# Expert rows loaded from GpSimd's queue, scatters without waits on each other, and the last block's low parts on VectorE

## The chip, the cores and the metric

The kernel runs on one core of a Trainium2 chip. The metric is the device time of one execution in microseconds (us). Engine names follow the profile: PE is TensorE's matmul stream (PEld its weight loads), DVE is VectorE, ACT is ScalarE, POOL is GpSimd, SP is SyncE, which does no arithmetic here and only issues transfers (SPq is its queue of instructions).

## The reference

Three layers follow each other on 3072 tokens of width 512:

```python
x  = attention(q, k, v)            # 4 batches, 8 heads, 768 tokens, head width 64, local window and global keys
h  = x @ w_in                      # 512 -> 2048
x  = (h - tanh(h)) @ w_out         # 2048 -> 512
e  = argmax(x @ w_gate, axis=1)    # each token goes to one of 8 experts
out[e == i] = gate_w * eom * (relu(x[e == i] @ w1[i]) @ w2[i])    # 512 -> 1024 -> 512
```

## The kernel before, in words

Every fp32 factor of a large matmul is held as a high and a low part, and each product is three matmuls (high by high, high by low, low by high), so most values that PE needs are written twice: the high part by ACT, the low part by a subtraction.

**First half.** The tokens go in 12 blocks of 256 (`blk` 0 to 11). For each block and each of 16 slices `u` of the hidden width, `moe_h` makes `ph` on PE, `gate` and `gate2` make `gg` on DVE and ACT, `parts` makes `gh` (ACT) and `gl` (line 645: DVE in block 0, POOL in all later blocks), and `moe_y` adds the slice into `y`. Attention of later blocks is woven in between. After a block its two halves of 128 rows are copied to `yrow` (buffers of the pool tag `row`, of which there are three), routed (`rt_logits`: `step1` to `step5`, with the rank matmuls `rk`, and the row numbers `su`), and written by `scatter` (line 793, an indirect DMA issued by POOL) to `srt`, a table in device memory that is sorted by expert. Each scatter of blocks 0 to 10 waits until the scatter before it has landed; the two of block 11 don't wait for each other.

**Second half.** `order_experts` ranks the experts by load, and nine jobs follow: job 0 is the first 256 rows of the fullest expert, which block 10 has already completed, job 1 its other 256 rows, and jobs 2 to 8 are the other experts, with 480 to 384 rows each. `ex_load` brings a piece of an expert's weights (`ex`, 512 KB, SP's queue, into the same `row` buffers), `ex_split` makes its high part `eh` on ACT (line 899) and its low part `el` on DVE (line 900). `ex_rows` (line 923) brings a job's sorted rows, `xr`, 128 at a time, on SP's queue too. `ex_T` turns them on PE (`xTp`, line 941) and splits them (`xTh` on ACT, `xTl` on DVE); `ex_s1` makes `h2p` and its parts `h2h` and `h2l`; `ex_s2` adds into `ob` (line 1000); `ex_out` scales `ob` to `orow` and POOL writes it to its places in `out` (line 1018, an indirect DMA).

**Order.** Each engine runs its instructions strictly in the order that the compiler of the kernel fixed beforehand, from the order of the code, ranks in an agenda and estimated times. An instruction that must wait therefore holds up all that stand behind it on its engine. This holds for SP's and POOL's transfers as well: a transfer that waits for a buffer or for another transfer keeps the next one from being issued.

Of the kernel before, what the change touches and what calls it, by code (L numbers as in the profile page):

```python
# [32 lines left out]
def kernel(  # L33
# [15 lines left out]
    nc = tc.nc  # L49
    P = 128  # L50
# [3 lines left out]
    E, _, F = w1.shape  # L54
    TB = 256
    NBLK = NT // TB
# [8 lines left out]
    RS = NT + CAP  # L65
# [14 lines left out]
    srt = dram.tile([E * RS, W], F32, name="srt")  # L80
# [11 lines left out]
    def bank(tag, bufs, name):  # L92
        t = psum.tile([P, 512], F32, tag=tag, bufs=bufs, name=name)
        return t
# [17 lines left out]
    order_i = persist.tile([P, E], I32, name="order_i")  # L112
# [19 lines left out]
    def at(gt, rank, fn):  # L132
        agenda.setdefault((gt, rank), []).append(fn)
# [465 lines left out]
    def moe_h(blk, u, gt):  # L599
        fg, fo = divmod(u, 4)  # L600
        ph = bank("h", 2, f"ph{blk}_{u}")
        n = 0
        for kc in range(KC):
            o = kc * 512 + fo * P
            whi, wlo = wih[fg][:, o : o + P], wil[fg][:, o : o + P]
            for lw, xx in ((whi, xhi), (whi, xlo), (wlo, xhi)):
                nc.tensor.matmul(ph[:, 0:TB], lw, xx[blk][:, kc, :], start=(n == 0), stop=(n == 3 * KC - 1))  # L607
                n += 1

        def tmp(tag, bufs, dt=F32):  # L610
            t = p1.tile([P, TB], dt, tag=tag, bufs=bufs, name=f"{tag}{blk}_{u}")
            return t

        L = {}

        def gate():
            hps = ph[:, 0:TB]
            uu = L["uu"] = tmp("uu", 2)
            ss = L["ss"] = tmp("ss", 2)
            tt = L["tt"] = tmp("tt", 2)  # L620
            vv = L["vv"] = tmp("vt", 2)
            nc.scalar.activation(uu, hps, AF.Square)  # L622
            nc.scalar.activation(tt, hps, AF.Tanh)  # L623
            nc.scalar.activation(ss, uu, AF.Square, scale=G_S, bias=ga[:, 0:1])  # L624
            nc.vector.scalar_tensor_tensor(out=vv, in0=uu, scalar=G_C, in1=hps, op0=ALU.add, op1=ALU.mult)  # L625
            nc.vector.tensor_tensor(out=tt, in0=tt, in1=hps, op=ALU.subtract)  # L626
            nc.vector.scalar_tensor_tensor(out=vv, in0=ss, scalar=G_S2B, in1=vv, op0=ALU.add, op1=ALU.mult)

        def gate2():
            uu, ss, tt, vv = L["uu"], L["ss"], L["tt"], L["vv"]  # L630
            gg = L["gg"] = tmp("gg", 2)
            if blk < 1:
                nc.scalar.activation(ss, uu, AF.Relu, bias=nt2[:, 0:1])
            else:
                nc.vector.tensor_scalar(out=ss, in0=uu, scalar1=G_T2, scalar2=None, op0=ALU.is_gt)
            nc.vector.tensor_tensor(out=gg, in0=vv, in1=uu, op=ALU.mult)
            nc.vector.copy_predicated(gg, ss.bitcast(I32), tt)  # L637

        def parts():
            gg = L["gg"]  # L640
            gh = tmp("gh", 3, F32R)
            gl = tmp("gl", 3, F32R)
            nc.scalar.copy(gh, gg)  # L643
            by = nc.vector if blk < 1 else nc.gpsimd
            by.tensor_tensor(out=gl, in0=gg, in1=gh.bitcast(F32), op=ALU.subtract)  # L645
            g_t[blk, u] = (gh, gl)

        at(gt + 1, 0, gate)
        at(gt + 2, 0, gate2)
        at(gt + 3, 0, parts)  # L650

    def moe_y(blk, u):
# [14 lines left out]


    rts = {}
    last_rows = []  # L670

    def rt_evac(blk):
        for j in range(2):
# [24 lines left out]
    def rt_logits(blk, gt):  # L698
# [92 lines left out]
        def scatter(j):  # L791
            r = rts.pop((blk, "row", j))
            store = nc.gpsimd.indirect_dma_start(
                out=srt[:, :], out_offset=IndirectOffsetOnAxis(ap=L["su"][:, j : j + 1], axis=0),
                in_=r[:, 0:W], in_offset=None, bounds_check=E * RS - 1, oob_is_err=False,
            )
            if blk == NBLK - 1:
                last_rows.append(store.ins)
                if j == 1:
                    tc.declare_no_dep(last_rows[1], last_rows[0], reason="each token has one row")  # L800

        last = blk == NBLK - 1
        rk = -2 if last else 0
# [4 lines left out]
        at(gt + 3, rk, step4)  # L808
        at(gt + 3, rk, step5)
        at(gt + 4, rk, lambda: scatter(0))  # L810
        at(gt + (4 if last else 6), rk, lambda: scatter(1))

    def plan_route(blk, gt):
# [21 lines left out]
    ordering = {}  # L835
# [25 lines left out]
        nc.vector.tensor_scalar(out=kk, in0=kk, scalar1=-1.0, scalar2=float(E), op0=ALU.mult, op1=ALU.add)  # L861
        nc.vector.tensor_copy(order_i, kk)

    def expert(r):

        if r not in ordering:
            ordering[r] = nc.values_load(
                order_i[0:1, r : r + 1], engines=[mybir.EngineType.SP], min_val=0, max_val=E - 1
            )
        return ordering[r]  # L870


    w1h, w1l, w2h, w2l = {}, {}, {}, {}
# [3 lines left out]
    def ex_load(e, i):  # L877
        st = rowt(f"ex{e}_{i}")
        rv = expert(e)
        if i < 4:  # L880
            nc.sync.dma_start(st, w1[ds(rv, 1), i * P : (i + 1) * P, :].rearrange("o p f -> p (o f)"))
        else:
            r = (i - 4) * 2 * P
            nc.sync.dma_start(
                st.rearrange("p (c d) -> p c d", c=2),
                w2[ds(rv, 1), r : r + 2 * P, :].rearrange("o (c p) d -> p (o c) d", p=P),
            )
        staged["e", e, i] = st
# [24 lines left out]
    def job_tile(n, tag, shape, dt, name):  # L913
        pool, tag, bufs = pools[tag, 0 if n == 0 else 2 - n % 2]
        t = pool.tile(shape, dt, tag=tag, bufs=bufs, name=name)
        return t

    def ex_rows(n):
        r, j0, _ = jobs[n]
        rv = expert(r)  # L920
        for j, m in tiles(n):
            t = job_tile(n, "xr", [P, W], F32, f"xr{n}_{j}")
            nc.sync.dma_start(t[0:m, :], srt[ds(rv * RS + (j0 + j) * P, m), :])
            xrows[n, j] = t

    def tiles(n):

        return [(j, min(P, jobs[n][2] - j * P)) for j in range((jobs[n][2] + P - 1) // P)]
# [259 lines left out]
    for i in range(NP):  # L1188
# [5 lines left out]
        ("orow", 0): (persist, "row", 3),  # L1194
    })
    at(G + 26, 0, lambda: ex_rows(0))
    for g in range(n_groups(0)):
        at(G + 28 + g, 4, lambda g=g: ex_T(0, g))
# [48 lines left out]
    for k in range(1, 3):  # L1247
        pools["hh", k] = p2, "h2h", 3
        pools["hl", k] = p2, "h2l", 3
        pools["orow", k] = p2, "orow", 4  # L1250

    ex_rows(1)
    for g in range(n_groups(1)):
        ex_T(1, g)
    for n in range(1, len(jobs)):
        e = jobs[n][0]
        for f in range(NF2):
            ex_s1(n, f)
            if n == 1:
                for i in range(NP):  # L1260
                    if steps[i] - NF2 == f:
                        ex_load(1, i)
                    if steps[i] + 2 - NF2 == f and i >= 4:
                        ex_split(1, i)
            elif e + 1 < E:
                ex_load(e + 1, f)
                if f >= 1:
                    ex_split(e + 1, f - 1)
            if f >= 1:
                if n < len(jobs) - 1 or f - 1 < NF2 - LATE:  # L1270
                    ex_s2(n, f - 1)
            elif n > 1:
                ex_s2(n - 1, NF2 - 1)
                ex_out(n - 1)
            if n + 1 < len(jobs):
                if f == 2:
                    ex_rows(n + 1)
                if 4 <= f < 4 + n_groups(n + 1):
                    ex_T(n + 1, f - 4)
                if f == NF2 - 1 and n > 1:  # L1280
                    ex_split(e + 1, NP - 1)
# [95 lines left out]
def build(shapes):  # L1377
    import numpy as _np
    import concourse.bacc as _bacc
    import concourse.tile as _tile  # L1380
    from concourse import mybir as _mybir

    nc = _bacc.Bacc("TRN2", target_bir_lowering=False, num_devices=1)
    args = []
    for name in _INS:
        shape, dtype = shapes[name]
        args.append(
            nc.dram_tensor(f"in_{name}_dram", shape, _mybir.dt.from_np(_np.dtype(dtype)), kind="ExternalInput").ap()
        )
    for i, (shape, dtype) in enumerate(_OUTS):  # L1390
        dt = _mybir.dt.from_np(_np.dtype(dtype))
        args.append(nc.dram_tensor(f"out_{i}_dram", shape, dt, kind="ExternalOutput").ap())
    with _tile.TileContext(nc, schedule_with_timeline_sim=True) as tc:
        kernel(tc, *args)
    return nc
# [23 lines left out]
```

## Time and profile before

| | |
|---|---|
| three runs | 1169.68, 1170.34, 1171.40 us (median 1170.34) |
| profiled execution, its own time | 1168.82 us |
| its span, first to last instruction | 1167.1 us |
| busy in the span | PE 1106.7, DVE 856.2, ACT 671.6, POOL 214.2 us |
| mean granted TensorE clock | 0.988 of 2.4 GHz |

The profile is of one execution, and its times count from the start of the span. The first half ends at about 815 us and the second follows up to 1155 us. A row of the timeline gives start, duration, engine, source line, operation, output <- inputs, and in square brackets how long the engine had been idle before it and what ended that. A granted clock of 1.00 is 2.4 GHz and 0.50 is 1.2 GHz.

### The profile page before, as it was taken

How to read it: one execution, taken by the hardware profiler on the slowest of the kernel's cores; microseconds unless marked ns; L12 is line 12 of the kernel's file. 1: busy time of each engine (PE TensorE's matmuls, PEld its weight loads, DVE VectorE, ACT ScalarE, POOL GpSimd, SP SyncE). 2: the span in 40 equal slices, each digit the busy share in tenths (PEclk: the TensorE clock that was granted, in tenths of full speed). 3: DMA queues.
4: the chain of work that ended last, by engine and by line, in shares of the span. 5: the costliest groups of instructions: out<-in, count | busy, mean ns of one | idle time of the engine just before them, and what ended most of it. 6: DMA issues, size and time to landing. Idle time of an engine off the chain costs nothing. (4 is left out here: it accounts for less than half of the span.)

```text
span 1167.1 us, 22211 instructions
## 1 busy us (share of the span) xinstructions
PE 1106.7 (95%) x7374; PEld 943.5 (81%) x7374; DVE 856.2 (73%) x2704; ACT 671.6 (58%) x1794; POOL 214.2 (18%) x281
## 2 busy tenths in 40 slices
PE   2888999999999999999999999998999999999995
PEld 1457888888888888888888888886888787888894
DVE  6899778899989889989889898998554434424411
ACT  4999876666666656666666666565352423423411
POOL 1000013222222222222222232324100100101100
PEclk9889999999999999999999999999999999999998
DMA  6954921111211112121112120113372614526200
GB/s 170 291 165 142 254 58 42 30 51 30 55 38 40 37 39 52 31 55 27 51 24 56 37 53 22 33 67 127 113 246 103 206 53 153 181 61 222 79 23 25
DMA packets 128850, 103.25 MB, mean 88 GB/s; under 512 B 101679, under 2 KB 101679, under 8 KB 128720
## 3 DMA queue, kind: packets, MB, share of 16 engines
q1 hardware_dynamic: 124592, 89.06, 26.7%
q0 software_dynamic: 4128, 12.61, 2.8%
q8 instruction: 62, 1.02, 0.4%
q14 instruction: 68, 0.56, 0.2%
HBM read 90.04 MB, written 21.88 MB: 96 GB/s over the span
## 5 line engine op out<-in xcount | busy, mean ns | idle before, releaser
L645 POOL TENSOR_TENSOR gl<-gg,gh 128x256 fp32r<-128x256 f32 x176 | 149.1, 847 | 485.7 <-ACT gh L643 368.1
L607 PE MATMUL ph<-xhi,wh 128*128 128x256 f32 x768 | 219.9, 289 | 3.5 <-DVE tt L626 3.5
L607 PE MATMUL ph<-xhi,wl 128*128 128x256 f32 x768 | 218.2, 285 | 0.0
L607 PE MATMUL ph<-xlo,wh 128*128 128x256 f32 x768 | 216.2, 282 | 0.0
L662 PE MATMUL y<-wh,gh 128*128 128x512 f32 x384 | 158.2, 412 | 1.0 <-ACT gh L643 0.9
L607 PEld LDWEIGHTS ph<-xhi,wh 128*128 128x128 f32 x768 | 144.8, 189 | 15.9 <-DVE tt L626 5.9
L662 PE MATMUL y<-wl,gh 128*128 128x512 f32 x384 | 154.1, 401 | 0.0
L607 PEld LDWEIGHTS ph<-xlo,wh 128*128 128x128 f32 x768 | 145.0, 189 | 6.7
L607 PEld LDWEIGHTS ph<-xhi,wl 128*128 128x128 f32 x768 | 144.8, 189 | 4.3 <-issue 2.6
L662 PE MATMUL y<-wh,gl 128*128 128x512 f32 x384 | 141.8, 411 | 2.5 <-POOL gl L645 2.3
L643 ACT CAST gh<-gg 128x256 fp32r<-128x256 f32 x192 | 78.2, 407 | 84.9 <-DVE gg L637 66.4
L622 ACT ACTIVATE uu<-ph 128x256 f32<-128x256 f32 x192 | 73.8, 384 | 78.3 <-PE ph L607 70.8
L978 DVE SCALAR_TENSOR_TENSOR h2l<-h2p,h2h 128x448 fp32r<-128x448 f32 (+3 forms) x72 | 40.0, 557 | 103.9 <-ACT h2h L977 103.8
L522 ACT ACTIVATE pr<-pr,sst 128x256 f32<-128x256 f32 (+1 forms) x192 | 93.0, 487 | 38.2 <-DVE sst L514 38.2
L625 DVE SCALAR_TENSOR_TENSOR vt<-uu,ph 128x256 f32<-128x256 f32 x192 | 79.8, 416 | 43.9 <-ACT tt L623 42.6
L900 DVE TENSOR_TENSOR el<-ex,eh 128x1024 fp32r<-128x1024 f32 x64 | 77.7, 1223 | 46.1 <-ACT eh L899 42.2
L977 ACT ACTIVATE h2h<-h2p 128x448 fp32r<-128x448 f32 (+3 forms) x72 | 35.3, 492 | 124.8 <-PE h2p L973 123.9
L899 ACT CAST eh<-ex 128x1024 fp32r<-128x1024 f32 x64 | 66.5, 1050 | 60.2 <-DMA ex<-in_moe_w_dram 45.0
L624 ACT ACTIVATE ss<-uu,ga 128x256 f32<-128x256 f32 x192 | 99.3, 517 | 0.0
L973 PE MATMUL h2p<-xTh,eh 128*128 128x448 f32 (+3 forms) x288 | 97.7, 342 | 0.0
L973 PE MATMUL h2p<-xTl,eh 128*128 128x448 f32 (+3 forms) x288 | 97.2, 338 | 0.0
L973 PE MATMUL h2p<-xTh,el 128*128 128x448 f32 (+3 forms) x288 | 97.1, 338 | 0.0
(199 smaller groups left out, 2505.6 us busy)
## 6 DMA issues: line engine op xcount, KB each, us to landing
ex<-in_moe_w_dram SPq DMA_DIRECT2D x64, 512.0 KB
vv<-vg SPq DMA_DIRECT2D x92, 96.0 KB
srt<-zrow SPq DMA_DIRECT2D x32, 257.0 KB
m<-in_moe_w_in_dram SPq DMA_DIRECT2D x16, 512.0 KB
m<-in_moe_w_out_dram SPq DMA_DIRECT2D x16, 512.0 KB
xr<-srt SPq DMA_DIRECT2D x25, 257.0 KB
qk<-in_q_dram SPq DMA_DIRECT2D x92, 64.0 KB
qk<-in_k_dram SPq DMA_DIRECT2D x92, 64.0 KB
```

The costliest lines, as they stand in the source:

```text
L522: nc.scalar.activation(pr[j][:, c0:], pr[j][:, c0:], AF.Exp, bias=st[:, j : j + 1], scale=-1.0, accum_out=st[:, 2 + j : 3 + j],)
L607: nc.tensor.matmul(ph[:, 0:TB], lw, xx[blk][:, kc, :], start=(n == 0), stop=(n == 3 * KC - 1))
L622: nc.scalar.activation(uu, hps, AF.Square)
L624: nc.scalar.activation(ss, uu, AF.Square, scale=G_S, bias=ga[:, 0:1])
L625: nc.vector.scalar_tensor_tensor(out=vv, in0=uu, scalar=G_C, in1=hps, op0=ALU.add, op1=ALU.mult)
L643: nc.scalar.copy(gh, gg)
L645: by.tensor_tensor(out=gl, in0=gg, in1=gh.bitcast(F32), op=ALU.subtract)
L662: nc.tensor.matmul(yb[blk, j], gx[:, j * P : (j + 1) * P], wx[fg][:, sl], start=(u == 0 and n == 0), stop=(u == NF - 1 and n == 2),)
L899: nc.scalar.copy(hi, st)
L900: nc.vector.tensor_tensor(out=ld[e, t][:, sl], in0=st, in1=hi.bitcast(F32), op=ALU.subtract)
L973: nc.tensor.matmul(ph[:, 0:N], lw, xx, start=(i == 0), stop=(i == 3 * KC - 1))
L978: nc.vector.scalar_tensor_tensor(out=hl, in0=ph[:, 0:N], scalar=0.0, in1=hh.bitcast(F32), op0=ALU.max, op1=ALU.subtract)
```

## The change

Three edits. The low part `gl` of the last block goes from POOL to DVE. All scatters into `srt` are put in one group whose members don't wait for each other. The loads `xr` of sorted rows are issued by POOL instead of SP, for which POOL also loads the eight expert numbers into registers.

```diff
-            by = nc.vector if blk < 1 else nc.gpsimd
+            by = nc.vector if blk in (0, NBLK - 1) else nc.gpsimd
             by.tensor_tensor(out=gl, in0=gg, in1=gh.bitcast(F32), op=ALU.subtract)
...
-            if blk == NBLK - 1:
-                last_rows.append(store.ins)
-                if j == 1:
-                    tc.declare_no_dep(last_rows[1], last_rows[0], reason="each token has one row")
+
+            tc.declare_no_dep(store.ins, group="srt", reason="each token has one row")
+            tc.add_to_no_dep_group("srt", store.ins)
...
-    def expert(r):
-
-        if r not in ordering:
-            ordering[r] = nc.values_load(
-                order_i[0:1, r : r + 1], engines=[mybir.EngineType.SP], min_val=0, max_val=E - 1
-            )
-        return ordering[r]
+    def expert(r, by=mybir.EngineType.SP):
+
+        if (r, by) not in ordering:
+            ordering[r, by] = nc.values_load(order_i[0:1, r : r + 1], engines=[by], min_val=0, max_val=E - 1)
+        return ordering[r, by]
...
     def ex_rows(n):
         r, j0, _ = jobs[n]
-        rv = expert(r)
+        rv = expert(r, mybir.EngineType.Pool)
         for j, m in tiles(n):
             t = job_tile(n, "xr", [P, W], F32, f"xr{n}_{j}")
-            nc.sync.dma_start(t[0:m, :], srt[ds(rv * RS + (j0 + j) * P, m), :])
+            nc.gpsimd.dma_start(t[0:m, :], srt[ds(rv * RS + (j0 + j) * P, m), :])
             xrows[n, j] = t
```

The order of instructions moves at several places. The first is POOL's, from the scatters of block 10 to the rows of job 1. In a name the first number is the block or job and the second the half or tile (`xr1_0` is tile 0 of job 1); the number after the last underscore only counts. Before:

```order
L645 TENSOR_TENSOR gl11_11_13155<-gg11_11_13137,gh11_11_13154 128x256
L793 DMA srt_63<-yrow10_0_12628,su10_12976 28672x514
L645 TENSOR_TENSOR gl11_12_13198<-gg11_12_13180,gh11_12_13197 128x256
L793 DMA srt_63<-yrow10_1_12631,su10_12976 28672x514
L645 TENSOR_TENSOR gl11_13_13244<-gg11_13_13217,gh11_13_13243 128x256
L645 TENSOR_TENSOR gl11_14_13294<-gg11_14_13276,gh11_14_13293 128x256
L680 TENSOR_SCALAR yrow11_0_13379<-tok0_86 128x1
L645 TENSOR_TENSOR gl11_15_13318<-gg11_15_13313,gh11_15_13317 128x256
L680 TENSOR_SCALAR yrow11_1_13382<-tok0_86 128x1
L793 DMA srt_63<-yrow11_0_13379,su11_13514 28672x514
L793 DMA srt_63<-yrow11_1_13382,su11_13514 28672x514
L1018 DMA out_0_dram<-orow0_0_13634,ix0_13271 3072x512
```

The same stretch of POOL's order in the changed kernel:

```order
L792 DMA srt_63<-yrow10_0_12628,su10_12976 28672x514
L792 DMA srt_63<-yrow10_1_12631,su10_12976 28672x514
L919 ISA
L919 DMA xr0_0_13186<-srt_63 128x514
L919 ISA
L919 DMA xr0_1_13188<-srt_63 128x514
L679 TENSOR_SCALAR yrow11_0_13389<-tok0_86 128x1
L679 TENSOR_SCALAR yrow11_1_13392<-tok0_86 128x1
L792 DMA srt_63<-yrow11_0_13389,su11_13524 28672x514
L792 DMA srt_63<-yrow11_1_13392,su11_13524 28672x514
```

And the rows right behind those:

```order
L1014 DMA out_0_dram<-orow0_0_13644,ix0_13281 3072x512
L1014 DMA out_0_dram<-orow0_1_13649,ix0_13281 3072x512
L919 ISA
L919 DMA xr1_0_13679<-srt_63 128x514
L919 ISA
L919 DMA xr1_1_13681<-srt_63 128x514
L919 ISA
L919 DMA xr2_0_13788<-srt_63 128x514
```

What moved: the subtractions have left POOL, the two scatters of block 10 stand next to each other, and the loads of job 1's rows, which were SP's, stand behind the writes of job 0's output.

The second place is PE's order where job 0 ends and job 1 begins. Before, the turning of job 1's rows stands ahead of job 0's last six output matmuls (those of `h2h0_7` and `h2l0_7`):

```order
L1000 MATMUL ob0_1_13396<-eh0_6_13131,h2l0_6_13588 128x512
L941 MATMUL xTp1_0_13673<-ident_66,xr1_0_13669 128x128
L941 MATMUL xTp1_1_13682<-ident_66,xr1_0_13669 128x128
L941 MATMUL xTp1_0_13673<-ident_66,xr1_1_13671 128x128
...
L1000 MATMUL ob0_0_13395<-eh0_6_13131,h2l0_7_13611 128x512
L1000 MATMUL ob0_1_13396<-eh0_6_13131,h2l0_7_13611 128x512
L973 MATMUL h2p1_0_13695<-xTh1_0_13678,eh0_0_12810 128x256
```

In the changed kernel it stands behind the last of them:

```order
L996 MATMUL ob0_0_13405<-eh0_6_13131,h2l0_7_13621 128x512
L996 MATMUL ob0_1_13406<-eh0_6_13131,h2l0_7_13621 128x512
L937 MATMUL xTp1_0_13683<-ident_66,xr1_0_13679 128x128
L937 MATMUL xTp1_1_13692<-ident_66,xr1_0_13679 128x128
L937 MATMUL xTp1_0_13683<-ident_66,xr1_1_13681 128x128
...
L937 MATMUL xTp1_1_13692<-ident_66,xr1_1_13681 128x128
L969 MATMUL h2p1_0_13705<-xTh1_0_13688,eh0_0_12810 128x256
L969 MATMUL h2p1_1_13724<-xTh1_0_13688,eh0_0_12810 128x256
L937 MATMUL xTp2_0_13846<-ident_66,xr2_0_13788 128x128
```

What moved: the eight turning matmuls of job 1 went past job 0's last six output matmuls, and the first one of job 2 now follows job 1's first two `h2p` matmuls. Further up in the same order the rank matmuls `rk` of block 11 went from behind `h2p0_4` to behind `h2p0_7`, so that 12 output matmuls of job 0 remain after them. At the end of block 11 PE's order has job 0's turning matmuls behind `gl11_13` instead of `gh11_15`. On DVE the `gl` of block 11 stand between the other gate steps, each two to five instructions behind its `gg`. On ACT the high part of `ex1_0`, the first piece of the next expert, now stands ahead of `gh11_14`. From SP's order all 29 loads `xr` are gone; its other rows keep theirs.

## Rows read from the trace of the kernel before

**Rows 1.** Busy us of each engine by stretch, then granted clock, DMA share, GB/s
```profile
core 0: us, PE busy (x) PEld busy (x) DVE busy (x) ACT busy (x) POOL busy (x), PEclk, DMA share, GB/s
600.00:700.00 100.00, 99.44 (x781) 87.52 (x780) 90.57 (x330) 63.67 (x197) 26.50 (x34) 1.00 0.18 45
...
800.00:820.00 20.00, 15.15 (x87) 11.42 (x86) 15.55 (x33) 10.31 (x21) 9.32 (x9) 1.00 0.40 133
```

**Rows 2.** Timeline: PE's two longest waits between 800 and 820 us
```profile
809.41 0.73 PE L662 MATMUL y<-wh,gl 128*128 128x512 f32 x2 [1.67 <-POOL gl L645]
...
814.63 0.41 PE L941 MATMUL xTp<-ident,xr 128*128 128x128 f32 x2 [1.66 <-DMA xr<-srt]
```

**Rows 3.** Timeline: block 10's scatters, job 0's loads
```profile
802.71 1.21 POOL L793 DMA_INDIRECT srt<-yrow,su  x1 [0.16 <-DVE tt L626]
...
806.58 1.73 POOL L793 DMA_INDIRECT srt<-yrow,su  x1 [1.88 <-DMA srt<-yrow,su]
...
811.80 0.91 SPq L923 DMA_DIRECT2D xr<-srt  x2
```

**Rows 4.** Timeline: block 11's rank and scatters, job 1's rows, job 0's end
```profile
830.47 0.18 PE L762 MATMUL rk<-ohb,tri 128*128 128x8 bf16 x1
...
832.34 0.17 DVE L787 CAST su<-sf 128x2 uint32<-128x2 f32 x1
...
833.37 1.08 POOL L793 DMA_INDIRECT srt<-yrow,su  x1 [19.52 <-DVE su L787]
834.75 0.98 POOL L793 DMA_INDIRECT srt<-yrow,su  x1 [0.30 <-issue]
...
837.91 0.88 SPq L923 DMA_DIRECT2D xr<-srt  x2
...
840.60 0.15 DVE L960 COPY so<-xr 128x1 f32<-128x1 f32 x1 [2.94 <-DMA xr<-srt]
...
840.78 0.38 PE L941 MATMUL xTp<-ident,xr 128*128 128x128 f32 x2
...
841.32 0.88 PE L941 MATMUL xTp<-ident,xr 128*128 128x128 f32 x6 [0.16 <-DMA xr<-srt]
...
841.90 1.07 ACT L954 CAST xTh<-xTp 128x512 fp32r<-128x512 f32 x2 [1.94 <-PE xTp L941]
841.95 0.48 PE L1000 MATMUL ob<-eh,h2h 128*128 128x512 f32 x1
...
842.97 0.63 PE L1000 MATMUL ob<-eh,h2l 128*128 128x512 f32 x2
...
844.37 0.97 POOL L1018 DMA_INDIRECT out_dram<-orow,ix  x1 [8.63 <-ACT orow L1013]
845.64 0.97 POOL L1018 DMA_INDIRECT out_dram<-orow,ix  x1 [0.30 <-issue]
```

**Rows 5.** Landing of POOL's transfers: scatters into srt, then writes of out
```profile
DMA to landing us min/median/max: 2.8/3.4/3.9
...
DMA to landing us min/median/max: 3.0/5.4/6.2
```

**Rows 6.** What SP's queue waited for, 840 to 1160 us: total, times, longest
```profile
SPq L923 <- PE xTp L941: 114.7, 7, 26.6
```

**Rows 7.** Timeline: PE's two long waits after 860 us
```profile
965.90 0.50 PE L1000 MATMUL ob<-eh,h2h 128*128 128x512 f32 x1 [1.77 <-ACT h2h L977]
...
1055.65 0.50 PE L1000 MATMUL ob<-eh,h2h 128*128 128x512 f32 x1 [1.73 <-ACT h2h L977]
```

**Rows 8.** By source line: durations min/median/max in ns
```profile
L645 DVE TENSOR_TENSOR gl<-gg,gh x16: 408/419/427, 84.1 to 145.3; 128x256 fp32r<-128x256 f32 x16
...
L635 DVE TENSOR_SCALAR ss<-uu x176: 267/293/1151, 147.5 to 808.8; 128x256 f32<-128x256 f32 x176
```

**Rows 9.** The same, SP's register loads of expert numbers
```profile
L867 SPq TENSOR_LOAD <-order_i x8: 262/262/280, 751.7 to 755.7; - x8
```

**Rows 10.** Busy time by stretch as in rows 1, where the clock fell
```profile
45.00:50.00 5.00, 2.77 (x16) 1.93 (x15) 4.94 (x17) 5.00 (x15) 0.00 (x0) 1.00 1.04 329
50.00:55.00 5.00, 4.40 (x13) 1.82 (x11) 3.80 (x10) 5.00 (x14) 0.00 (x0) 0.56 1.02 338
```

More of the change, by code (lines that the diff above doesn't have):

```diff
@@ L669 @@
     rts = {}
-    last_rows = []
     def rt_evac(blk):
```

## The prediction, made before the changed kernel ran

> **What bounds the kernel now.** I began with the busy time of each engine by stretch. From 600 to 700 us PE is busy for 99.44 of 100 us at full clock [rows 1]: there another engine's work is worth nothing unless PE comes to wait for it. The same view from 800 to 820, where the first half hands over to the second, shows PE busy for 15.15 of 20 us [rows 1], so 4.85 us are open. The timeline of PE in that stretch says what ended the idle time: its two longest waits are 1.67 us on a `gl` of POOL and 1.66 us on job 0's rows `xr`, by DMA [rows 2]; the rest of the 4.85 is in shorter ones. After 860 us the timeline has only two long waits of PE, 1.77 and 1.73 us, both on ACT's `h2h` [rows 7]. So what can be won is 4.85 + 1.77 + 1.73 = 8.35 us, and everything else that the change does can only cost. I therefore looked at the place where the order makes PE wait for something new: the border of job 0 and job 1.
>
> **The border of jobs 0 and 1: +9.6 us.** Before, the rank matmul `rk` of block 11 runs at 830.47, its row numbers `su` are written at 832.34, the two scatters start at 833.37 and 834.75, so 2.9 and 4.3 us after `rk`; SP issues job 1's rows at 837.91, the last rows are there when the second group of turning matmuls starts at 841.32, and job 0's last six output matmuls run from 841.95 until 842.97 + 0.63 = 843.60 [rows 4]. The turning was 841.95 - 840.78 = 1.2 us of PE's time with work of job 0 on both sides, and `h2p` of job 1 follows at once at 843.60.
>
> In the changed order `rk` stands 12 output matmuls ahead of the end of job 0 (call the end E), and job 1's turning behind E. Output matmuls start (842.97 - 841.95) / 4 = 0.255 us apart [rows 4], so `rk` starts 12 x 0.255 = 3.1 us ahead of E. From there:
>
> - the first scatter starts at E - 3.1 + 2.9 = E - 0.2, the second at E - 3.1 + 4.3 = E + 1.2;
> - behind it POOL issues, one after the other, two writes of job 0's output and two loads of job 1's rows. The two writes of before start 845.64 - 844.37 = 1.27 us apart [rows 4]. A write can't start until 844.37 - 843.60 = 0.77 us after E, which is past by then. At 1.27 each the writes start at E + 2.5 and E + 3.75, the loads at E + 5.0 and E + 6.3;
> - the loads also need the landed scatters: 3.4 us at the median [rows 5] from E + 1.2, so E + 4.6, which is hidden by the two writes;
> - landing of the second load: POOL loads no plain rows in the trace of before, so this is bounded. Below stands SP's load of the same rows, issued at 837.91 and first used at 840.60, 2.7 us [rows 4]; above, POOL's writes of `out`, 5.4 us at the median. I take the 3.4 of POOL's transfers with `srt` [rows 5], which move the same rows the other way: E + 9.7;
> - from the arrival of the last rows to `h2p`: the matmuls at 841.32 feed a cast of `xTh` at 841.90 that takes 1.07 us for two, 0.53 for one [rows 4], so 841.90 + 0.53 - 841.32 = 1.1 us: E + 10.8.
>
> Before, `h2p` came at E with the 1.2 us of turning already spent, so the loss is 10.8 - 1.2 = **9.6 us**. PE has nothing to do meanwhile: what follows in its order is job 1's own `h2p`. With the landing of 2.7 the loss is 8.9, with 5.4 it is 11.6. If the scatters of block 11 were out of the way (an earlier `rk`), the writes would start at E + 0.77 and all that follows 1.7 us sooner, 7.9, and with the short landing too 7.2. If a POOL transfer occupies its engine for longer, there are five steps in a row: the scatter at 806.58 takes 1.73 us [rows 3] against the 0.97 of those I used, so 5 x 0.76 = 3.8 us more, 13.4.
>
> The Trainium skill says in "SBUF — State Buffer", section "Who interferes with whom", that VectorE and GpSimd share one pair of ports as an exclusive lock, and that a transfer whose descriptors GpSimd writes stalls while VectorE holds it. The row of 1.73 us agrees with that without proving it; by that rule the loss is the 13.4, by the other rows 9.6.
>
> **What is late next: +0.5.** Pieces of the next expert's weights stand between job 1's steps on ACT and DVE, and loads of weights use the same `row` buffers as the scatters and writes, so some of them come later too. That SP or ACT is stuck so shows in the two `h2h` waits of 1.77 and 1.73 [rows 7]; nothing shows it for this place, so 0 to 2 us, nearest to nothing as POOL's writes land before the rows of job 1 do.
>
> **The clock: +1.0.** The granted clock is 1.00 in a stretch in which PE was busy for 2.77 of 5 us, and 0.56 in the next 5 us [rows 10], so mostly at 1.2 instead of 2.4 GHz. A gap of 9.6 us is longer than any that I saw in the second half. If the same follows here, 5 x (1 - 0.56) = 2.2 us of full-speed work is lost; if the clock holds, nothing. I take about half.
>
> **The handover at 800 to 820: -1.5.** The 16 `gl` of block 11 take 0.419 us each on DVE, as block 0's do, 6.7 us in all [rows 8]. DVE is busy for 90.57 of 100 us in the blocks before [rows 1], so it takes some 70 us until it has as much free time. What makes up for it is POOL's absence: DVE's `ss` take 0.293 us at the median and up to 1.151 [rows 8], as neighbours of POOL's own work. I reckon it out even: DVE is no freer at the end of block 11. The wait of 1.67 on POOL's `gl` then goes, but a DVE that is behind gives a part of it back. The scatters of block 10 no longer wait for each other: the second starts one step after the first, at 802.71 + 1.27, about 804, in place of 806.58 [rows 3]. SP's load starts at 811.80 [rows 3]; POOL's could start after the landing (3.4) and one step, at about 809, and its rows come some 2 us sooner, which is the wait of 1.66 on `xr` [rows 2]. Against that ACT now makes a weight piece ahead of `gh11_14`, for which DVE's `gl` waits. Bounds 0 and -4.85; I take a third of the hole, -1.5, since each of its waits has another close behind it.
>
> **Later jobs: -2.5.** SP's queue stands with a load `xr` at its head waiting for the turning of an earlier job (`xTp`, whose buffers it takes) for 114.7 us in 7 waits, the longest 26.6 [rows 6]. Weight loads stand behind it, ACT's high parts behind those, and `h2h` behind them. With `xr` on POOL the weights are free to go. Both `h2h` waits, 3.5 us, can go; I take 2.5, as weights wait for their own buffers as well. POOL's own loads of later jobs are issued a job ahead and cost nothing; if one of them held up a write of `out`, no later step would need that write soon. The register loads, 262 ns each on SP [rows 9], are now eight more on POOL in a time in which its subtractions are gone: the scatter of block 11 had 19.52 us of idle time before it [rows 4]. If they weren't covered, it would be 8 x 0.262 = 2.1 us, but only two stand ahead of the border's loads and two among them, so 0 to 0.5, taken as 0.
>
> The Trainium skill says in "DMA: Bandwidth & Descriptors", section "Issuing engines are not separate DMA queues", that issuing from several engines saves only the time of initiating a transfer. By that the later jobs gain nothing; the 114.7 us of waiting at the head of SP's queue say otherwise.
>
> **Sum.** 9.6 + 0.5 + 1.0 - 1.5 - 2.5 = +7.1 us. The profiled execution took 1168.82 us, 1.7 more than its span of 1167.1; it would take 1175.9. The three runs' median, 1170.34, stands 1.5 above it, so **1177.4 us**.
>
> **Rivals.**
>
> 1. POOL's transfers take long: the border costs 13.4 in place of 9.6, +3.8, which makes 1181.2. For it speaks the row of 1.73 us [rows 3]; against it that DVE has little to do while PE stands, so the four rows around 0.97 to 1.08 [rows 4] are nearer.
> 2. The weights aren't helped: loads wait for the `row` buffers in any case, the two waits on `h2h` [rows 7] stay, and the sum is +9.6, 1179.9. For it speaks that the waits are only two in nine jobs; against it the 114.7 us at SP's head [rows 6].
> 3. Not slower: the transfers at the border are quick and the holes close. The loss there is then 7.2 (no scatters ahead, landing of 2.7), clock and weights cost nothing, and all 8.35 us of waits go: 7.2 - 8.35 = -1.2, so 1169.2. It decides where the loss at the border falls under 8.35 us. Against it: it needs PE without a pause from 800 to 820, and `rk` earlier than the order has it.
> 4. The move does nothing at the border, because POOL's loads are in time anyway. Then only the gains remain, -4.0, 1166.3. Against it: the loads stand behind the writes of job 0's output in POOL's order, and those need the end of job 0.
>
> **How the numbers follow.** Chances: the forecast 0.55, rival 1 0.17, rival 2 0.13, rival 3 0.10, rival 4 0.05. About 0.2% (2.3 us) is what a measurement of this kernel can tell from no change, so "same" is 1168.0 to 1172.7. Rival 3 lies in it, rival 4 is faster; with the corners of the forecast (a full hole gained, a border of 8.9) same is 0.11, faster 0.06 and slower 0.83. The range goes from 1171.5, which is the forecast with a border of 7.9, no clock loss and 3.2 us more won at the holes (7.1 - 1.7 - 1.0 - 3.2 = +1.2), to 1183.5, rival 1 with a clock loss of 2.2 and weights later by another 1.1; what lies outside, half of rival 3, rival 4 and the far end of rival 1, is under 2 in 10.
>
> **What the profile of the changed kernel would show.** Right: PE idle for about 9 to 10 us between the last `ob` of job 0 and the turning of job 1, ended by the DMA of `xr`; ahead of it on POOL two scatters, two writes, two loads in steps near 1.3 us; a lower granted clock in the 5 us after it; 800 to 820 with PE busy for about 16.5 of 20 us; no wait on `h2h` near 965 and 1055. Wrong: a gap under 5 us (POOL's steps or landing shorter than any row here), loads that start before the writes of `out`, steps of 2 us (rival 1), or new waits of PE after 900 us for rows that POOL loads too late, which I have costed at nothing.

## The result, and the profile after

The changed kernel took 1182.38 us (median of 4 runs, 1180.86 to 1183.07) beside 1170.87 for the kernel before in the same comparison: a ratio of 1.0083, 95% interval 1.0066 to 1.0100, so 11.5 us slower. The profiled execution has a span of 1180.6 us, 13.5 more than before. Of that 1.2 is there already at 184 us, ahead of the first scatter (the first rank matmul runs at 185.03 instead of 183.81), and 1.1 at 678 us (the rank matmuls of block 9 run at 678.92 instead of 677.78); this late start is no part of the change.

Busy time by stretch, as in [rows 1] and [rows 10]; the second and the last two rows are the ones in which the clock fell:

```profile
core 0: us, PE busy (x) PEld busy (x) DVE busy (x) ACT busy (x) POOL busy (x), PEclk, DMA share, GB/s
800.00:820.00 20.00, 14.19 (x69) 10.93 (x69) 15.25 (x39) 8.91 (x19) 5.06 (x6) 0.83 0.48 159
812.23:819.06 6.83, 5.24 (x18) 4.29 (x19) 4.97 (x13) 2.90 (x5) 0.26 (x1) 0.50 0.39 136
845.00:850.00 5.00, 0.34 (x2) 0.00 (x0) 0.75 (x1) 0.69 (x1) 3.60 (x5) 0.98 0.42 158
850.00:855.00 5.00, 0.00 (x0) 0.00 (x0) 0.72 (x1) 1.04 (x1) 2.19 (x4) 0.50 0.84 310
855.00:860.00 5.00, 4.04 (x16) 3.24 (x17) 2.89 (x9) 2.19 (x3) 1.08 (x2) 0.50 1.04 389
```

PE has no work at all from 850 to 855, and the 4 us of work after that run at the lower clock. The handover from 800 to 820 has got worse too, 14.19 us busy instead of 15.15, and 5.24 of these at the lower clock. The timeline at both places, to set beside [rows 2 to 4]:

```profile
801.02 2.45 POOL L792 DMA_INDIRECT srt<-yrow,su  x1 [37.99 <-ACT tt L623]
...
803.78 0.97 POOL L792 DMA_INDIRECT srt<-yrow,su  x1 [0.31 <-issue]
...
808.75 0.59 POOL L919 DMA_DIRECT2D xr<-srt  x1 [4.00 <-DMA srt<-yrow,su]
...
813.43 0.66 PE L937 MATMUL xTp<-ident,xr 128*128 128x128 f32 x2 [4.34 <-DMA xr<-srt]
...
842.38 0.18 PE L762 MATMUL rk<-ohb,ones_bf 128*128 128x8 bf16 x1
...
844.51 1.12 POOL L792 DMA_INDIRECT srt<-yrow,su  x1 [31.23 <-DVE ext_f L1233]
...
844.72 0.63 PE L996 MATMUL ob<-eh,h2l 128*128 128x512 f32 x2
...
845.93 0.99 POOL L792 DMA_INDIRECT srt<-yrow,su  x1 [0.30 <-issue]
...
847.22 0.97 POOL L1014 DMA_INDIRECT out_dram<-orow,ix  x1 [0.30 <-issue]
...
848.99 0.97 POOL L1014 DMA_INDIRECT out_dram<-orow,ix  x1 [0.80 <-DVE orow L1011]
...
849.30 6.61 SPq L880 DMA_DIRECT2D ex<-in_moe_w_dram  x4
849.96 2.24 POOL L919 DMA_DIRECT2D xr<-srt  x4
...
855.92 2.14 PE L937 MATMUL xTp<-ident,xr 128*128 128x128 f32 x8 [10.58 <-DMA xr<-srt]
...
856.52 1.14 PEld L937 LDWEIGHTS xTp<-ident,xr 128*128 128x128 f32 x6 [0.34 <-DMA xr<-srt]
...
858.10 0.80 PE L969 MATMUL h2p<-xTh,eh 128*128 128x256 f32 x2
```

Job 0 ends at E = 844.72 + 0.63 = 845.35; the order on POOL (two scatters, two writes, then the loads) is the one of the forecast, and PE stands for 10.58 us until `xr` of job 1 has landed. What PE waited for after 860 us answers to [rows 7]: the two long waits on `h2h` are gone.

```profile
PE h2p L969 <- DVE ix L957: 0.9, 1, 0.9
PE ob L996 <- ACT h2h L973: 0.6, 1, 0.6
```

### The profile page after: what moved, and what is told of

It is laid out like the page before. It is cut to its first block, busy times and chain, and to the rows that moved or that the text cites. A ratio compares the mean times of both kernels' runs of the same rounds, so it can differ in the third digit from the quotient of the medians.

```text
span 1180.6 us, 22262 instructions
## 1 busy us (share of the span) xinstructions
PE 1107.0 (94%) x7374; PEld 945.7 (80%) x7374; DVE 851.7 (72%) x2720; ACT 671.5 (57%) x1794; POOL 220.4 (19%) x294
## 4 chain that ended last, share of the span: by engine, by line
PE 80%; DVE 6%; ACT 4%; issue 4%; DMA 3%; POOL 1%; SPq 0%; POOLq 0%; DVEq 0%; ACTq 0%
PE y L662 22%; PE ph L607 20%; PE ob L996 12%; PE h2p L969 11%; PE xp L560 4%; PE sc L497 4%; PE pt L546 3%; PE xTp L937 1%; PE pk L433 1%; PE yT L688 1%; DMA ex<-in_moe_w_dram 1%; DMA vv<-in_v_dram 1%; DVE gg L636 1%; PE lp L703 1%; PE pq L430 1%
## 5 line engine op out<-in xcount | busy, mean ns | idle before, releaser
L645 POOL TENSOR_TENSOR gl<-gg,gh 128x256 fp32r<-128x256 f32 x160 | 131.6, 822 | 487.1 <-ACT gh L643 357.5
L996 PE MATMUL ob<-eh,h2h 128*128 128x512 f32 x232 | 92.5, 399 | 0.6 <-ACT h2h L973 0.6
```

What stands on the lines that cost most here:

```text
L996: nc.tensor.matmul(ob[n, j][0:m, :], gx[:, j * P : j * P + m], wx, start=(f == 0 and i == 0), stop=(f == NF2 - 1 and i == 2),)
```

## The experiments

Theory 1 is the prediction's: job 1's rows come late because POOL issues them behind two writes, so the third edit makes the loss. Theory 2 came from the order of instructions: what is late is the rank matmul `rk` of block 11. All that job 1 needs hangs on it (row numbers, scatters, loads, turning), and PE's order decides how much work of job 0 is left behind it to cover that chain. Each run was timed in five rounds against the kernel before.

**Each edit alone, and two together.** `low_only` has the first edit of the change alone:

```diff
-            by = nc.vector if blk < 1 else nc.gpsimd
+            by = nc.vector if blk in (0, NBLK - 1) else nc.gpsimd
```

> The kernel before with the first edit alone: the low parts of block 11 on DVE; loads of rows stay on SP. Theory 1 (the prediction's): the border of jobs 0 and 1 is lost because POOL's loads of job 1's rows stand behind two writes; here they are on SP, so at most 3 us are lost, 1170 to 1174 us. Theory 2 (the rival, from the order of instructions): with the low parts on DVE block 11's logits and rank matmuls get a later place in PE's order, 12 output matmuls and 5 h2p matmuls ahead of the end of job 0 (3.7 us) instead of 13, so its scatters can't land before job 0 ends, on whichever queue the loads are: PE idle for about 8 to 9 us there, and 1178 to 1182 us.

Measured: 1183.49 against 1171.85, ratio 1.0110 (1.0085 to 1.0136). One edit, with all loads on SP, makes as large a loss as all three, a little more than theory 2 expected. Its timeline at the handover and at the border:

```profile
810.21 1.04 ACT L899 CAST eh<-ex 128x1024 fp32r<-128x1024 f32 x1 [4.10 <-DMA ex<-in_moe_w_dram]
...
811.62 0.80 PE L662 MATMUL y<-wh,gh 128*128 128x512 f32 x1 [5.61 <-ACT gh L643]
...
842.11 0.18 PE L763 MATMUL rk<-ohb,ones_bf 128*128 128x8 bf16 x1
...
844.46 0.63 PE L1000 MATMUL ob<-eh,h2l 128*128 128x512 f32 x2
...
845.72 0.97 POOL L793 DMA_INDIRECT srt<-yrow,su  x1 [0.30 <-issue]
...
849.32 0.88 SPq L923 DMA_DIRECT2D xr<-srt  x2
...
850.54 1.08 SPq L884 DMA_DIRECT2D ex<-in_moe_w_dram  x2
...
852.44 0.66 PE L941 MATMUL xTp<-ident,xr 128*128 128x128 f32 x2 [7.36 <-DMA xr<-srt]
...
854.86 0.79 PE L973 MATMUL h2p<-xTh,eh 128*128 128x256 f32 x2
```

The second scatter starts only after job 0 has ended (845.09), and SP's load can't be issued until it has landed. Theory 1, as the account of the whole loss, falls here. The loss is made up otherwise than in the changed kernel, though: the wait at the border is 7.36 us instead of 10.58, but PE's waits on `h2h` behind it add up to 6.1 us, where the changed kernel has 0.6.

`rows_only` has the third edit alone:

```diff
-            nc.sync.dma_start(t[0:m, :], srt[...])
+            nc.gpsimd.dma_start(t[0:m, :], srt[...])
```

> The kernel before with the third edit alone: the loads of rows issued by POOL. Theory 1: PE waits at the border for POOL's loads, 1176 us or more. Theory 2: the rank matmuls keep their early place, POOL's loads of job 1 stand directly behind the scatters of block 11, the border costs nothing and the two waits on h2h after 900 us are gone: 1165 to 1168.5 us.

Measured: 1176.75, ratio 1.0040 (1.0023 to 1.0057). The time is the one that theory 1 expected, but not for its reason: at the border PE waits 1.83 us for `xr`, while the first rows of job 0 are late, and PE waits 5.94 us for them at 820.38. Theory 2 misses the time.

`scat_only` has the second edit alone:

```diff
-            if blk == NBLK - 1:
...
+            tc.declare_no_dep(store.ins, group="srt", reason="each token has one row")
+            tc.add_to_no_dep_group("srt", store.ins)
```

> The kernel before with the second edit alone: scatters without waits on each other. Theory 1: nothing lost at the border, up to 1.7 us won at the handover: 1168 to 1171 us. Theory 2: the rank matmuls stand some 7 us ahead of the end of job 0 and the turning of job 1 behind it, so the scatters land about when job 0 ends and SP's load and the turning follow: PE idle for about 4 us at the border, 1172 to 1176 us.

Measured: 1177.03, ratio 1.0048 (1.0033 to 1.0063), 1 us above theory 2's range, with waits of 3.40 and 0.23 us on `xr` at the border. A change of scatters alone moved `rk` too:

```profile
834.71 0.17 PE L763 MATMUL rk<-ohb,ones_bf 128*128 128x8 bf16 x1
...
841.25 0.63 PE L998 MATMUL ob<-eh,h2l 128*128 128x512 f32 x2
...
847.74 0.80 PE L971 MATMUL h2p<-xTh,eh 128*128 128x256 f32 x2
```

`rows_scat` is the changed kernel with the first edit undone:

```diff
-            by = nc.vector if blk in (0, NBLK - 1) else nc.gpsimd
+            by = nc.vector if blk < 1 else nc.gpsimd
```

> The changed kernel without the first edit: the low parts of block 11 stay on POOL, loads on POOL and free scatters as changed. Theory 1: the loads on POOL cost the border, 1175 us or more. Theory 2: the rank matmuls are at their early place again and the loads of job 1 stand directly behind block 11's scatters, no wait over 2 us at the border, handover and later jobs gain up to 5: 1164 to 1169 us, faster than before.

Measured: 1174.95, ratio 1.0025 (1.0011 to 1.0038). Most of the loss is gone, but the time lies at the lower edge of what theory 1 expected and doesn't speak against it. The border does: PE waits 2.03 us for `xr` there instead of 10.58, with the loads on POOL (ahead of the writes here, since `rk` is early). That it would be faster than before was wrong as well. The handover loses: job 0's first `h2p` starts at 819.83 instead of 816.77, with a wait of 2.30 us on POOL's `xr` among others.

`scat_low` is the changed kernel with the third edit undone, `rows_low` with the second:

```diff
# scat_low
-            nc.gpsimd.dma_start(t[0:m, :], srt[...])
+            nc.sync.dma_start(t[0:m, :], srt[...])
# rows_low
-            tc.add_to_no_dep_group("srt", store.ins)
+            if blk == NBLK - 1:
...
```

> The changed kernel without its third edit: all rows are loaded by SP as before; low parts of block 11 on DVE and free scatters as changed. The rank matmuls have their late place, 3.7 us ahead of the end of job 0. If POOL's loads make the loss: 1174 us or less. If the late rank matmuls make it: 1180 to 1184 us, as with the first edit alone.

> The changed kernel without its second edit: the scatters of blocks 0 to 10 wait for each other again; low parts on DVE and rows on POOL as changed, rank matmuls late. If the free scatters are worth what the forecast took for the handover, it is 1 to 2 us slower than the changed kernel (1183 to 1185); if they are worth nothing once the rank matmuls are late, it is within 1 us of it.

Measured: `scat_low` 1183.52 against 1172.25, ratio 1.0095 (1.0075 to 1.0114); `rows_low` 1185.65, ratio 1.0109 (1.0087 to 1.0131). Taking the loads off POOL, the prediction's culprit, gives nothing back in time. At the border it does, where `scat_low` waits 6.94 us instead of 10.58; but with all rows on SP again, PE's waits on `h2h` behind it are 7.9 us in its profile. In `rows_low` the median is 3 us above the changed kernel's, but the ratios' intervals overlap: what the free scatters are worth stays open.

**The place of `rk` alone.** `rank_late` is the kernel before with block 11's logits and rank planned later, and nothing else:

```diff
-            at(gt + 5, -2, lambda: rt_logits(blk, gt + 5))
+            at(gt + 17, 4, lambda: rt_logits(blk, gt + 17))
...
-        rk = -2 if last else 0
+        rk = 4 if last else 0
...
+        gt += 6 if last else 0
```

> The kernel before, with none of the three edits: only the logits, rank matmuls and row numbers of block 11 are planned later, so that the last rank matmul stands 6 us ahead of the end of job 0 instead of 13; loads stay on SP. Theory 2: the second scatter starts some 1.7 us ahead of the end of job 0 and lands 2.3 after it, SP's load adds 3.2, turning and cast 1.1, so PE stands about 5 us and the time is 1175 to 1179 us. Rival (the place of the rank matmuls is only a sign of something else): no gap, 1169 to 1173 us.

Measured: 1178.67 against 1169.78, ratio 1.0074 (1.0049 to 1.0100).

```profile
837.13 0.18 PE L763 MATMUL rk<-ohb,ones_bf 128*128 128x8 bf16 x1
...
842.44 0.63 PE L1001 MATMUL ob<-eh,h2l 128*128 128x512 f32 x2
...
843.77 0.87 SPq L924 DMA_DIRECT2D xr<-srt  x2
...
846.53 0.59 PE L942 MATMUL xTp<-ident,xr 128*128 128x128 f32 x2 [3.46 <-DMA xr<-srt]
...
849.45 0.80 PE L974 MATMUL h2p<-xTh,eh 128*128 128x256 f32 x2
```

From the end of job 0 (843.07) to job 1's `h2p` it is 6.4 us, less 1.2 of turning 5.2; expected were about 5. The place of `rk` alone opens the gap. It isn't the whole of the 8.9 us by which this kernel is slower. Behind the border PE works 6.04 us at half the clock, which loses 3.0, and its waits on `h2h` add up to 6.1 us instead of 3.5. Its busy time where the clock fell:

```profile
846.62:853.45 6.83, 6.04 (x25) 5.02 (x26) 2.78 (x6) 2.65 (x4) 0.00 (x0) 0.50 0.97 322
```

`el_pool` keeps all three edits and takes other work off DVE, by which `rk` returns to its place behind `h2p0_4`:

```diff
-        nc.vector.tensor_tensor(out=ld[e, t][:, sl], in0=st, ...)
+        (nc.gpsimd if e == 0 and i >= 4 else nc.vector).tensor_tensor(out=ld[e, t][:, sl], in0=st, ...)
```

> The changed kernel with all three edits, and the low parts of weight pieces 4 to 7 of the first expert on POOL instead of DVE: by that the rank matmuls of block 11 are back at their early place (behind h2p0_4, 13 us ahead of the end of job 0) and the loads of job 1's rows stand on POOL directly behind the scatters, ahead of the writes of job 0's output. Theory 2 (the late place of the rank matmuls is what costs the border): no wait of over 3 us between job 0 and job 1, 1169 to 1175 us. Rival (the low parts on DVE cost as such, by DVE's time, or the loads on POOL by POOL's steps): a gap of 7 us or more stays, 1179 us or more.

Measured: 1178.02, ratio 1.0063 (1.0041 to 1.0085), between the two expectations. The border closes: the only wait on `xr` left there is 1.87 us. But a low part of a weight piece takes 2.40 us on POOL (1.23 on DVE), the handover waits for ACT's `gh` 3.6 us and for `gl` 2.5, and PE's waits for `h2h` after that add up to 4.2.

**The queue of the loads.** `job1_sp` is the changed kernel with job 1's rows alone back on SP, `later_pool` the kernel before with jobs 2 to 8 on POOL, `jobs1to8_pool` with jobs 1 to 8 on POOL, `job0_pool` with job 0 alone on POOL. All have one edit in `ex_rows`, with conditions of `n == 1`, `n < 2`, `n == 0` and `n > 0` (the first is shown, against the changed kernel):

```diff
+        on_sp = n == 1
...
-            nc.gpsimd.dma_start(t[0:m, :], srt[...])
+            (nc.sync if on_sp else nc.gpsimd).dma_start(t[0:m, :], srt[...])
```

> The changed kernel with one thing undone: the rows of job 1 are loaded by SP again, all other rows by POOL; the rank matmuls keep their late place, 3 us ahead of the end of job 0. If the place of POOL's loads behind two writes costs what the prediction counted (2.5 us of steps and a longer landing), the gap of 10.6 us shrinks to about 7.5 and the time is 1178 to 1180.5 us. If the late rank matmuls alone set it, it stays over 9.5 us and the time within 1 us of the changed kernel's.

Measured: 1180.76, ratio 1.0093 (1.0065 to 1.0121): by its ratio no better than the changed kernel. The gap did shrink, from 10.58 to 6.56 us, and by more than the prediction's account gives (to about 7.5), so the late `rk` doesn't set it alone. But the kernel got little of it back in time, because now more of the work behind it runs at the lower clock (the border, then the same view as above; here PE is busy and the clock at 0.50):

```profile
840.16 0.18 PE L762 MATMUL rk<-ohb,ones_bf 128*128 128x8 bf16 x1
...
842.50 0.62 PE L997 MATMUL ob<-eh,h2l 128*128 128x512 f32 x2
...
852.13 0.80 PE L970 MATMUL h2p<-xTh,eh 128*128 128x256 f32 x2
```

```profile
850.00:855.00 5.00, 4.76 (x20) 3.79 (x18) 0.91 (x3) 1.25 (x2) 1.09 (x2) 0.50 1.03 384
855.00:860.00 5.00, 4.43 (x20) 4.02 (x20) 3.42 (x9) 2.77 (x4) 0.00 (x0) 0.50 0.86 284
```

> The kernel before with one change: the rows of jobs 2 to 8 are loaded by POOL; those of jobs 0 and 1 stay on SP, and the order of instructions is that of before until the end of job 0. If SP's waiting loads hold up the weights, the two waits on h2h near 965 and 1055 us go and it takes 1166 to 1169 us. If issuing from another engine saves nothing, 1170 to 1172 us.

Measured: 1167.34 against 1169.78, ratio 0.9975 (0.9959 to 0.9991). This is the part of the change that is worth having, and the one version here that beats both kernels. PE's waits after 860 us, then ACT's for weight pieces in the same stretch, before and in this kernel (total, times, longest):

```profile
PE ob L1000 <- ACT h2h L977: 1.5, 4, 0.8
ACT eh L899 <- DMA ex<-in_moe_w_dram: 27.9, 23, 5.3
ACT eh L898 <- DMA ex<-in_moe_w_dram: 10.1, 12, 2.5
```

The weights do come sooner. SP's queue still stands, now for 118.2 and 62.2 us at weight pieces whose own buffers are still read by `el`, so the 114.7 us of [rows 6] were no measure of what could be won.

> The kernel before with the rows of jobs 1 to 8 loaded by POOL, those of job 0 by SP: the rank matmuls of block 11 keep their early place, and POOL's loads of job 1 stand directly behind the two scatters, ahead of the writes of job 0's output. If rows on POOL cost the border as the prediction held, PE waits 3 us or more for them there: 1171 us or more. If the late rank matmuls are what costs it, the loads start some 4 us ahead of the end of job 0, land about 5 us after their issue as in the runs so far, PE waits 1 to 2 us, and the gain of the later jobs is kept: 1167 to 1170 us.

Measured: 1170.90 against 1170.97, ratio 0.9999 (0.9986 to 1.0011), between the two expectations. The wait decides: with an early `rk` POOL's loads of job 1 cost 1.38 us at 842.81, as theory 2 said, not 3 or more. But the gain of the later jobs is gone, with that wait and with 3.6 us of waits on `h2h`.

> The kernel before with only the rows of job 0 loaded by POOL, all others by SP: the loads stand on POOL behind a small step of block 11 (the token numbers into yrow11) that waits until a scatter of block 10 has landed and freed its buffer. If that place and POOL's longer landing are what the handover lost with rows on POOL, PE waits for xr0 some 4 to 6 us and the time is 1174 to 1177 us; if the transfers are hidden there, 1170 to 1172 us.

Measured: 1175.33, ratio 1.0043 (1.0027 to 1.0059), as expected. The wait is 3.70 us, a little short of the 4 to 6, and the place makes it: from the first load's start to the turning it is 3.1 us, no longer than by SP. The small POOL step that waits for a scatter, the loads behind it, and PE:

```profile
812.34 0.22 POOL L680 TENSOR_SCALAR yrow<-tok 128x1 f32<-128x1 f32 x1 [3.81 <-DMA srt<-yrow,su]
...
813.03 0.63 POOL L923 DMA_DIRECT2D xr<-srt  x1 [0.48 <-issue]
...
816.15 0.66 PE L941 MATMUL xTp<-ident,xr 128*128 128x128 f32 x2 [3.70 <-DMA xr<-srt]
```

## Why the prediction came out as it did

The sign and the range were right, the size was short: +11.5 us measured, +7.1 forecast. That the time still fell into the range is in part luck: its upper end was put there for long POOL steps (rival 1), which didn't come, and nothing in it stood for a handover that gets worse. Step by step:

**The border: +9.6 forecast, 845.35 to 858.10 less 1.2 of turning = 11.55 in the profile.** The working holds up to the writes: scatters at E - 0.84 and E + 0.58 (forecast E - 0.2 and E + 1.2), writes at E + 1.9 and E + 3.6 (E + 2.5 and E + 3.75). Three terms were mis-sized. Loads follow each other in 0.56 us, not in the 1.27 of the indirect writes, so the second started at E + 5.2 instead of E + 6.3. Landing of the two took 5.8 and 5.9 us, above the upper bound of 5.4, where 3.4 was taken; the second landed at about E + 11.1 instead of E + 9.7:

```profile
DMA to landing us min/median/max: 5.8/5.9/5.9
```

From there (the weight load at 856.52 waits for it) to `h2p` it was 1.6 us instead of 1.1, at the lower clock.

**What it was put down to was wrong in the main.** The prediction gave the border to POOL's queue. The number of output matmuls behind `rk` stood in its working, but not that this number was the change's main effect, nor which edit made it. Eight profiles make it plain; E is the end of the last `ob` of job 0:

| kernel | last `rk` to E | E to job 1's `h2p` | sum | loads of job 1 |
|---|---|---|---|---|
| before | 12.7 | -0.2 | 12.5 | SP |
| scat_only | 7.2 | 5.9 | 13.0 | SP |
| rank_late | 5.9 | 6.4 | 12.3 | SP |
| low_only | 3.0 | 9.8 | 12.8 | SP |
| scat_low | 3.0 | 9.6 | 12.6 | SP |
| job1_sp | 3.0 | 9.0 | 12.0 | SP |
| after | 3.0 | 12.7 | 15.7 | POOL, behind the writes |
| rows_low | 3.0 | 13.0 | 15.9 | POOL, behind the writes |

The ends of the row for the kernel before (the end of its job 0 is in [rows 4]):

```profile
830.88 0.18 PE L763 MATMUL rk<-ohb,ones_bf 128*128 128x8 bf16 x1
...
843.44 0.40 PE L973 MATMUL h2p<-xTh,eh 128*128 128x256 f32 x2
```

From `rk` to `h2p` of job 1 it takes 12 to 13 us by SP, in whichever kernel. The kernel before has just that much work of job 0 behind `rk`, so PE doesn't wait and its sum is the upper end of what the chain can have taken there; work that is moved ahead of `rk` is lost at the border.

With the loads on POOL behind the writes it takes 3 to 4 us more, and that is the size of the prediction's culprit. Little of it is the place behind the writes: the first load starts 4.0 us after the second scatter (845.93 to 849.96), where SP's first load starts 3.0 to 3.6 us after it in the kernels of the table. Most of it is the landing, 6.0 us from the first load's start to the turning against 2.8 to 3.1 by SP. Whether POOL's queue makes that or the weight pieces do isn't shown: in the changed kernel SP issues pieces just ahead of the loads (849.30), in `low_only` behind them (850.54), and no run separates the two. In the time of `job1_sp` none of it is seen, since the clock takes most of it back.

Why the low parts on DVE move `rk` is only argued: with them DVE's planned work at the end of block 11 grows, so the block ends later in the plan, and `el_pool`, which takes work off DVE again, puts `rk` back. On the chip DVE was not what held it up: it is busy for 15.25 of 20 us at the handover, and PE waits 0.4 us for its `gl`.

**The handover: -1.5 forecast, about +1.8 measured.** This step failed by its sign: job 0 ends 2.95 us later than it should (845.35 against 843.60 less the 1.2 of turning that now come after it), of which 1.1 is the late start. The waits on POOL's `gl` did go, and the rows of job 0 came 1.2 us sooner (813.43 against 814.63), or 2.3 with the late start taken off, as forecast. But PE's order now has their turning ahead of the `y` matmuls of slices 14 and 15, of which before only the last two were left by then: a wait of 4.34 us in place of 1.66. In that wait the clock fell, and PE's next 5.24 us of work ran at 0.50 until 819.06; half of that, 2.6 us, is more than the whole 1.8. The forecast had counted the clock at the border alone. ACT's `gh11_14` came late too (814.76), behind weight pieces for which ACT itself had stood 3.15 and 2.18 us, so these matmuls could not have filled that wait as things stood. `low_only` has the same without POOL's loads: PE waits 5.61 us for ACT's `gh`, ACT 4.10 for a weight piece, and job 0 ends 2.7 us late. So the first edit makes a loss here by itself. `job0_pool`, 4.4 us slower, can't be set against it: its loads stand behind a POOL step that waits for a scatter and start at 813.03, in the changed kernel at 808.75.

**Clock, weights, later jobs: +1.0, +0.5 and -2.5 forecast, -1.2 together measured** (1180.6 - 858.10 = 322.5 us from job 1's `h2p` to the end, against 323.7). The clock stood at 0.50 for 4 us of PE's work, 2.0 us lost; a new wait of 0.9 on `ix` came behind a weight piece on DVE; the long waits on `h2h` went. `later_pool` gives the last by itself, 2.4 us (1.1 to 4.8 by its interval), which is the forecast. Late start, handover, border and this rest, 1.1 + 1.8 + 11.6 - 1.2 = 13.3, make up the 13.5 us of the two profiles to 0.2.

What `later_pool` moved is where the loads wait: on POOL's queue, no longer at the head of SP's. Its gain speaks against the rule of the Trainium skill, "DMA: Bandwidth & Descriptors", "Issuing engines are not separate DMA queues", as far as it was weighed: the time of initiating isn't all that another engine's queue saves.

**Rivals.** Rival 1 gave the nearest time (1181.2) by the wrong means: POOL's steps at the border weren't long, 0.97 to 1.12 us. One scatter was, 2.45 us at 801.02, while DVE was busy throughout; the next, at 803.78, took 0.97 us with DVE busy for 0.94 of it. The Trainium skill says in "SBUF — State Buffer", section "Who interferes with whom", that a transfer issued by GpSimd can be stalled by VectorE over the ports that they share. These two rows don't decide whether that happened here, and no run isolates it. Rival 2 falls with the time of `later_pool`, though it had one thing right: weight pieces do wait for their own buffers. Rival 3 is nowhere seen, and rival 4 fell with the gap of 10.58 us.

## What to carry to other kernels

When a change lets a planner place instructions anew, first find the long chain through the device's memory that a later stage hangs on, and count in the order how much work of the bound engine stands between the chain's first instruction and its end; here 12 to 13 us had to be covered and 3 were left. Undo each edit alone before blaming the one that does the late thing: the loads that PE waited for made 3 to 4 us of this gap, and an edit on another engine, a stage earlier, had made the rest. Freeing the queue that stood at its head was worth 2.4 us here, with the transfers alone that had slack (jobs 2 to 8); moving job 1's rows too took it back, and moving job 0's alone cost 4.4.

## What the runs showed of the hardware

How long the rows took to land went with what else was in flight, and not with the issuing engine alone. The list of transfers has a median from issue to landing for POOL's loads in the changed kernel (over those whose landing it shows):

```profile
xr<-srt POOLq DMA_DIRECT2D x25, 257.0 KB, 5.8
```

Four of them, at 870.80 to 873.91, landed faster:

```profile
DMA to landing us min/median/max: 2.6/3.3/3.7
```

The busy time in that stretch and in that of job 1's loads, to be read as above, shows the 16 DMA engines busy for 0.61 and 0.88 of it (the last number but one):

```profile
870.80:874.80 4.00, 4.00 (x25) 3.57 (x24) 1.21 (x3) 0.84 (x3) 2.16 (x4) 1.00 0.61 186
849.96:856.48 6.52, 0.56 (x2) 0.29 (x2) 1.70 (x4) 2.09 (x2) 2.23 (x5) 0.50 0.88 329
```

For SP the list has no median; the rows that PE waited for give 3.1 us from the first load's start to the turning in `low_only` (849.32 to 852.44) and 2.8 in `rank_late` (843.77 to 846.53). By the same measure POOL's take 6.0 in the changed kernel and 3.1 in `job0_pool` (813.03 to 816.15). That POOL's loads are slower as such is not shown.

In these runs the clock's fall is paid in work, not in waiting. In the changed kernel it fell during a gap of 10.6 us and held 0.50 for 4.0 us of work afterwards; after the shorter gap of 6.6 us in `job1_sp` PE worked 9.2 us at 0.50. So of the 4 us by which the gap was shorter, 2.6 (half of 9.2 less half of 4.0) went into slower work.
